# The short last slice of a dense layer: a bias written to PSUM by ScalarE and two row tiles for 64 features

## The chip, the cores and the metric

The kernel runs on one NeuronCore of a Trainium2 chip. The metric is the device time of one execution in microseconds (us), as the median of several runs. The engines are named as in the profile: PE is TensorE (matmuls), PEld its weight loads, ACT is ScalarE, DVE is VectorE, POOL is GpSimd and SP is SyncE, which issues most DMAs.

## What is computed

Two branches of the same input x (2048 tokens, D = 640 features) are mixed by a gate:

```
g = sigmoid((x * gate_w).sum(-1))                    # per token
a = 2*Re(C h_t) + x*Dskip,  h_t = L*h_(t-1) + B x_t  # complex diagonal recurrence, P = 640 states
b = gelu(x @ w1 + b1) @ w2 + b2                      # w1: 640 x 1728, w2: 1728 x 640
out = g*a + (1 - g)*b                                # bf16
```

The change is in the second product of b, `gelu(..) @ w2 + b2`. It sums over F = 1728 features, which are 13 slices of 128 and a last one of 64.

## The kernel before, in words

The tokens are worked in four quarters of 512 (q) and 16 chunks of 128 (c, four to a quarter). For each quarter the input stage makes, with matmuls of 512 columns (tokens), the 13 first-layer slices (`m1`, L640) and the ten B projections of the recurrence (`bproj`, L685), each a sum of five matmuls in one PSUM bank. ACT evicts a first-layer bank through the gelu into `Gl` (L648) and a B bank into `U` (L694). The last 64 features are made for two quarters at once by `m1_last` (L661): quarter q0 on output partitions 0 to 63, quarter q0+1 on 64 to 127, ten matmuls in all, and two gelus (L671) write them to rows 0 to 63 of two `GlL` tiles. Row 64 of each `GlL` holds ones.

DVE runs the recurrence in blocks of 256 tokens (`ssm(b)`: pre, scan, post), and post writes `H`, which holds two chunks. For each chunk then:

- `m2(c)`: the second layer in two halves of 320 columns, in banks 4 and 5. Each half is 13 matmuls of a `Gl` slice with w2 (L760) and one of `GlL` (L761), whose 65 rows are the 64 features and the ones; row 64 of the last w2 slice holds b2, so that this matmul also adds the bias. ACT evicts each half to `E1`, times 1 - g (L768).
- `cproj(c)`: the C projection, two halves of 320 columns in banks 6 and 7, ten matmuls of `H` with `CT` each (L786), which ACT evicts to `E2`, times g (L797). The last chunk has three pieces of 320, 192 and 128 columns and is finished by DVE straight from PSUM (L819).
- `comb(c)`: DVE adds x*Dskip*g (`xg`, L805), E1 and E2 (L489), and SP stores the result (L841).

`outs(q)` does this for the four chunks of a quarter, always `m2`, then `cproj`, then `comb`.

The order of the work on each engine is fixed when the program is built. A list scheduler (`Sched.order`) goes through time with an assumed cost for each step and takes, on the engine that is free first, the released step of the lowest `prio`; PE steps get rising numbers in program order. The cost is used for this order alone. Waits on semaphores are put in from the tiles and banks that steps read and write (`Prog.op`, `Emitter.wait`). Each engine then works through its own list strictly in order.

Banks: in the first two quarters the input stage goes round all eight banks (`in_bank`, L589), later round 0 to 3.

DMAs on SP's queue, in order: x for quarter 0, w1, b1, the B transposes, the xT transposes of quarter 1 (`xT1`), w2 in two pieces (`w2a`, 13 slices; `w2b`, the 64 rows; L579 and L580), the xT transposes of quarters 2 and 3 (`xT23`), and ten transposes of C (`CT`, L581). A reader of `CT` waits for all ten. On POOL's queue: b2 (one row, L852), Dskip and the gate weights (each repeated on 128 partitions), and x for later quarters.

Of the kernel before, what the change touches and what calls it, by code (L numbers as in the profile page):

```python
# [184 lines left out]
def bass_gated_mix__ssm_conv_s5__dense_activation_gelu__prompt_kernel(  # L185
# [40 lines left out]
    with ExitStack() as es, nc.Block() as block:  # L226

        def SB(name, shape, dt):
            return es.enter_context(nc.sbuf_tensor(name, list(shape), dt))
# [7 lines left out]
        Gl = [SB(f"Gl_{i}", [128, NF - 1, 512], BF16) for i in range(2)]  # L237
        GlL = [SB(f"GlL_{i}", [65, 512], BF16) for i in range(3)]
        dsk = SB("dsk", [128, D], BF16)
# [49 lines left out]
        BK_IN = [0, 1, 2, 3]  # L289
        BK_M2 = [4, 5]  # L290
        BK_C = [6, 7]
# [26 lines left out]
        def d_act(n):  # L318
            return 0.26 + n * 0.00084
# [68 lines left out]

        def f_ones():
            t = None  # L390
            for i in range(3):
                t = inc("dve", nc.vector.memset(GlL[i][64:65, :], 1.0))
            return t

        op("ones", "dve", 1.1, (), ["gl1"], f_ones, prio=-40)

# [182 lines left out]
        load("w2a", "sp", "l_w2a", W2sb[:, 0:NF - 1, :], B_w2[0:nmain, :].rearrange("(j p) d -> p j d", p=128), ["w2a"], prio=7.5, lat=8.0)  # L579
        load("w2b", "sp", "l_w2b", W2sb[0:FL, NF - 1, :], B_w2[nmain:F, :], ["w2b"], prio=7.6, lat=4.0)  # L580
        load_T("C", "l_C", [(CT[:, k, ci, :], (A_C_re, A_C_im)[ci][:, k * 128:(k + 1) * 128]) for k in range(KP) for ci in range(2)],  # L581
               ["CT"], prio=10, dur=14.0)

        ctr = {"in": 0, "pe": 0}

        def in_bank():
            i = ctr["in"]
            ctr["in"] += 1
            return (7 + i) % 8 if i < 2 * (NF - 1 + 2 * KP) + 1 - NW else BK_IN[i % 4]  # L589

# [62 lines left out]
        def m1_last(q0):  # L653
            jf = NF - 1
            bank = in_bank()

            def f_mm():
                t = None
                for k in range(KD):
                    for h in range(2):  # L660
                        t = nc.tensor.matmul(PS[bank][h * 64:(h + 1) * 64, :], W1sb[:, k, jf * 128:F],  # L661
                                             xT[:, k, (q0 + h) * 512:(q0 + h + 1) * 512], start=(k == 0), stop=(k == KD - 1))
                return inc("pe", t)

            op(f"m1_{q0}_{jf}", "pe", KD * d_mm(512) + 0.2, XT[q0] + XT[q0 + 1] + [("w1", "r")], [("bank", bank)], f_mm, prio=pe_prio())

            def f_ge():
                t = None
                for h in range(2):
                    ph = slice(h * 64, (h + 1) * 64)  # L670
                    t = inc("act", nc.scalar.activation(GlL[(q0 + h) % 3][0:64, :], PS[bank][ph, :], ACT.Gelu_apprx_tanh, bias=b1col[ph, jf:jf + 1]))  # L671
                return t

            op(f"ge_{q0}_{jf}", "act", 2 * d_act(512), [("bank", bank), "b1col"], [("glL", q0 % 3), ("glL", (q0 + 1) % 3)], f_ge, prio=10)

# [72 lines left out]


        def m2(c):  # L750
            q, t4 = c // 4, c % 4
            for hf in range(2):
                bank = BK_M2[hf]
                cols = slice(hf * HALF, (hf + 1) * HALF)

                def f_mm(bank=bank, cols=cols):
                    t = None
                    ts = slice(t4 * 128, (t4 + 1) * 128)
                    for jf in range(NF - 1):
                        t = nc.tensor.matmul(PS[bank][:, 0:HALF], Gl[q % 2][:, jf, ts], W2sb[:, jf, cols], start=(jf == 0), stop=False)  # L760
                    t = nc.tensor.matmul(PS[bank][:, 0:HALF], GlL[q % 3][0:FL + 1, ts], W2sb[0:FL + 1, NF - 1, cols], start=False, stop=True)  # L761
                    return inc("pe", t)

                op(f"m2_{c}_{hf}", "pe", NF * d_mm(HALF), [("gl", q % 2, jf) for jf in range(NF - 1)] + [("glL", q % 3), "gl1", "w2a", "w2b", "b2"],
                   [("bank", bank)], f_mm, prio=pe_prio())

                def f_ev(bank=bank, cols=cols):
                    return inc("act", nc.scalar.activation(E1[c % NE][:, cols], PS[bank][:, 0:HALF], ACT.Copy, scale=g1col[:, c:c + 1]))  # L768

                op(f"e1_{c}_{hf}", "act", d_act(HALF), [("bank", bank), ("g", q)], [("E1", c % NE, hf)], f_ev, prio=5)  # L770


        LAST = [(BK_C[0], 0, HALF), (BK_C[1], HALF, HALF + 192), (BK_M2[0], HALF + 192, D)]

# [70 lines left out]
        def outs(q):  # L845
            for c in range(4 * q, 4 * q + 4):
                m2(c)
                cproj(c)
                comb(c)

        m1_first()
        load("b2", "pool", "l_b2", W2sb[64:65, NF - 1, :], B_b2.rearrange("(o n) -> o n", o=1), ["b2"], prio=-30, dur=1.0, reads=["late"])  # L852
        load("dsk", "pool", "l_dsk", dsk[:, :], A_Dskip.partition_broadcast(128), ["dsk"], prio=-29, dur=1.0, reads=[("xT", 1)])
# [93 lines left out]
```

## Time and profile before

| | us |
|---|---|
| median of 3 runs | 217.36 (217.31 to 217.64) |
| profiled execution, its own time | 217.69 |
| its span, first to last instruction | 215.9 |
| PE busy | 212.0 (98% of the span) |
| DVE busy | 191.5 (89%) |
| ACT busy | 99.3 (46%) |
| 416 matmuls L760, 128x320: mean of one | 0.299 |
| 32 matmuls L761, 65x320: mean of one | 0.301 |
| 425 matmuls L640 and L685, 128x512: mean of one | 0.379 |
| gelu of a 128x512 bank (L648), one | 0.692 |
| eviction of 128x320 (L768), one | 0.528 |

Matmuls overlap in the pipeline, so the mean length of one is longer than the distance from one to the next; the distance is read from the chain of waits, which lists each stretch of the path with its start, its length and its number of instructions. The page has a strip of 40 slices for each engine, the groups of instructions by line, and the DMA issues; single stretches are read from the timeline. TensorE's granted clock is full (9 in each slice of the strip).

### The profile page before, as it was taken

The page shows a single profiled execution, that of the slowest core. Times are in us where ns is not written, and L with a number is a line of the kernel's source. Part 1 is how long each engine was busy: PE and PEld are TensorE (multiplying, and loading weights), DVE is VectorE, ACT ScalarE, POOL GpSimd, SP SyncE. Part 2 cuts the span into 40 slices and gives each one's busy share as a digit, 9 for nine tenths or more (in the row PEclk, how much of TensorE's full clock was granted, in tenths as well). Part 3 has the DMA queues.
Part 4 walks back from the last instruction along what each step waited for, and adds up shares of the span by engine and source line. Part 5 has one row for each costly group of instructions (what it writes and reads, how often), then busy time and mean ns, then how long its engine had stood idle before and what let it go on. Part 6 is the DMA issues. An engine that isn't in the chain of part 4 may idle for free.

```text
span 215.9 us, 3291 instructions
## 1 busy us (share of the span) xinstructions
PE 212.0 (98%) x1287; PEld 123.6 (57%) x1287; DVE 191.5 (89%) x269; ACT 99.3 (46%) x169; POOL 4.6 (2%) x13
## 2 busy tenths in 40 slices
PE   8899999999999999999999999999999999999995
PEld 3444444444567776444457777544447777777774
DVE  3989999999999999999996999799999999996313
ACT  2478556665533324556653322556662233233220
POOL 1010021000000100000000010000000000000000
PEclk9999999999999999999999999999999999999999
DMA  6987659996620050000000014000000000000000
GB/s 183 343 140 119 105 116 347 291 160 131 128 45 30 30 153 2 30 0 0 3 0 0 33 39 145 30 3 0 0 0 3 1 34 29 30 30 33 30 30 30
DMA packets 28201, 15.44 MB, mean 72 GB/s; under 512 B 22044, under 2 KB 27740, under 8 KB 28188
## 3 DMA queue, kind: packets, MB, share of 16 engines
q1 hardware_dynamic: 27598, 12.95, 25.4%
q0 software_dynamic: 560, 2.30, 3.4%
q8 instruction: 10, 0.16, 0.3%
q14 instruction: 3, 0.02, 0.0%
q10 hardware_dynamic: 30, 0.00, 0.0%
HBM read 7.38 MB, written 2.62 MB: 46 GB/s over the span
## 4 chain that ended last, share of the span: by engine, by line
PE 96%; DMA 2%; SPq 0%; DVE 0%; issue 0%
PE ps L760 26%; PE ps L640 22%; PE ps L786 20%; PE ps L685 20%; PE ps L621 4%; DMA W1sb<-in_B_w_dram 2%; PE ps L761 2%; PE ps L661 1%; SPq L330 0%; DVE osb L819 0%; PE ps L439 0%
## 5 line engine op out<-in xcount | busy, mean ns | idle before, releaser
L760 PE MATMUL ps<-W2sb,Gl 128*128 128x320 bf16 x416 | 61.4, 299 | 0.0
L760 PEld LDWEIGHTS ps<-W2sb,Gl 128*128 128x128 bf16 x416 | 40.6, 98 | 16.6 <-issue 0.4
L640 PE MATMUL ps<-xT,W1sb 128*128 128x512 bf16 x225 | 49.2, 379 | 0.0
L786 PE MATMUL ps<-CT,H 128*128 128x320 bf16 (+2 forms) x330 | 46.1, 295 | 0.0
L725 DVE TENSOR_TENSOR_SCAN W<-atab,V 128x1280 bf16<-128x1280 f32 x16 | 44.3, 2812 | 0.3
L685 PE MATMUL ps<-xT,BT 128*128 128x512 bf16 x200 | 43.8, 379 | 0.0
L786 PEld LDWEIGHTS ps<-CT,H 128*128 128x128 bf16 x330 | 31.7, 98 | 12.1 <-DMA CT<-in_A_C_im_dram 0.2
L648 ACT ACTIVATE Gl<-ps,b1col 128x512 bf16<-128x512 f32 x45 | 30.6, 692 | 16.1 <-PE ps L640 16.1
L640 PEld LDWEIGHTS ps<-xT,W1sb 128*128 128x128 bf16 x225 | 22.0, 98 | 26.6
L768 ACT ACTIVATE E<-ps,g1col 128x320 bf16<-128x320 f32 x32 | 16.9, 528 | 43.0 <-PE ps L761 43.0
L685 PEld LDWEIGHTS ps<-xT,BT 128*128 128x128 bf16 x200 | 19.5, 98 | 23.5 <-issue 0.4
L694 ACT ACTIVATE U<-ps 128x512 bf16<-128x512 f32 x40 | 23.9, 597 | 18.3 <-PE ps L685 18.3
L797 ACT ACTIVATE E<-ps,gcol 128x320 bf16<-128x320 f32 x30 | 15.8, 527 | 25.0 <-PE ps L786 25.0
L489 DVE TENSOR_TENSOR osb<-xg,E 128x640 bf16<-128x640 bf16 x15 | 7.3, 487 | 10.1 <-ACT E L797 10.0
L805 DVE SCALAR_TENSOR_TENSOR xg<-xn,gcol,dsk 128x640 bf16<-128x640 bf16 x16 | 13.9, 883 | 0.4
L600 DVE SCALAR_TENSOR_TENSOR scr<-xn,gwb 128x640 bf16<-128x640 bf16 x16 | 13.2, 822 | 0.4
L489 DVE TENSOR_TENSOR H<-H,V 128x1280 bf16<-128x1280 bf16 x16 | 12.5, 821 | 0.3
L489 DVE TENSOR_TENSOR V<-V,W 128x1280 bf16<-128x1280 bf16 x16 | 12.5, 821 | 0.3
L489 DVE TENSOR_TENSOR V<-mr,U 128x2560 bf16<-128x2560 bf16 x8 | 11.9, 1488 | 0.5 <-DVE s L489 0.2
L489 DVE TENSOR_TENSOR H<-c,W 128x2560 bf16<-128x2560 bf16 x8 | 11.9, 1488 | 0.1
L489 DVE TENSOR_TENSOR V<-s,W 128x2560 bf16<-128x2560 bf16 x8 | 11.9, 1484 | 0.0
L489 DVE TENSOR_TENSOR W<-mi,U 128x2560 bf16<-128x2560 bf16 x8 | 11.9, 1484 | 0.0
(84 smaller groups left out, 100.8 us busy)
## 6 DMA issues: line engine op xcount, KB each, us to landing
out_dram<-osb SPq DMA_DIRECT2D x15, 160.0 KB, 1.8
W2sb<-in_B_w_dram SPq DMA_DIRECT2D x1, 2080.0 KB, 12.6
xn<-in_A_x_dram POOLq DMA_DIRECT2D x3, 640.0 KB, 5.0
W1sb<-in_B_w_dram SPq DMA_DIRECT2D x5, 224.0 KB, 4.9
W1sb<-in_B_w_dram SPq DMA_DIRECT2D x1, 1040.0 KB, 7.8
xn<-in_A_x_dram SPq DMA_DIRECT2D x2, 320.0 KB, 3.4
xT<-in_A_x_dram SPq DMA_TRANSPOSE x10, 4.0
dsk<-in_A_Dskip_dram POOLq DMA_DIRECT2D x1, 160.0 KB, 6.8
```

The lines of the kernel that those rows point to most:

```text
L489: return inc("dve", nc.vector.tensor_tensor(out=o, in0=a, in1=b, op=o_))
L600: t = inc("dve", nc.vector.scalar_tensor_tensor(out=scr[:, :], in0=xn[q % 2][:, c, :], scalar=1.0, in1=gwb[:, :], op0=ALU.mult, op1=ALU.mu ...
L640: t = nc.tensor.matmul(PS[bank][:, :], W1sb[:, k, jf * 128:(jf + 1) * 128], xT[:, k, q * 512:(q + 1) * 512], start=(k == 0), stop=(k == KD ...
L648: return inc("act", nc.scalar.activation(Gl[q % 2][:, jf, :], PS[bank][:, :], ACT.Gelu_apprx_tanh, bias=b1col[:, jf:jf + 1]))
L685: t = nc.tensor.matmul(PS[bank][:, :], BT[:, kd, ci, k * 128:(k + 1) * 128], xT[:, kd, q * 512:(q + 1) * 512], start=(kd == 0), stop=(kd = ...
L694: return inc("act", nc.scalar.activation(dst, src, ACT.Copy, scale=1.0 if ci == 0 else -1.0))
L725: t = inc("dve", nc.vector.tensor_tensor_scan(out=g[:, ci, :], data0=a, data1=v[:, ci, :], initial=0.0, op0=ALU.mult, op1=ALU.add))
L760: t = nc.tensor.matmul(PS[bank][:, 0:HALF], Gl[q % 2][:, jf, ts], W2sb[:, jf, cols], start=(jf == 0), stop=False)
L768: return inc("act", nc.scalar.activation(E1[c % NE][:, cols], PS[bank][:, 0:HALF], ACT.Copy, scale=g1col[:, c:c + 1]))
L786: t = nc.tensor.matmul(PS[bank][:, 0:n], H[b % NHB][:, ci, k, s * 128:(s + 1) * 128], CT[:, k, ci, cols], start=(i == 0), stop=(i == 2 * K ...
L797: return inc("act", nc.scalar.activation(E2[c % NE][:, cols], PS[bank][:, 0:HALF], ACT.Copy, scale=gcol[:, c:c + 1]))
L805: return inc("dve", nc.vector.scalar_tensor_tensor(out=xg[c % 2][:, :], in0=xn[q % 2][:, c % 4, :], scalar=gcol[:, c:c + 1], in1=dsk[:, :] ...
```

## The change

- `GlL` becomes two tiles of 128 rows, one for two quarters. `m1_last` regroups the tokens: rows 0 to 63 get the first two chunks of both quarters, rows 64 to 127 the last two chunks of both. One gelu of 128 rows replaces the two.
- The bias is no longer a 65th row. b2 is loaded on 128 partitions (`b2b`), the rows of ones go, and ACT copies it into PSUM ahead of the matmuls (`seed`): the first 512 columns of the four chunks to banks 0 to 3, and the last 128 columns of two chunks each to banks 4 and 5. No second-layer matmul starts a sum of its own any more (`start=False`).
- The last w2 slice is loaded twice, on partitions 0 to 63 and 64 to 127 (`w2b0`, `w2b1`).
- For each quarter `m2_open` seeds the six banks and then runs the last 64 features of its four chunks (`m2l`): eight matmuls, alternately on array rows 0 to 63 and 64 to 127.
- `m2(c)` is the other 13 slices, in pieces of 512 and 128 columns instead of two of 320, and so are its evictions.
- In `outs(q)` the first chunk of each quarter has its C projection ahead of `m2_open` and `m2`.
- The input stage's last four banks of the first round become 0 to 3.

```diff
@@ -235,7 +235,8 @@
         BT = SB("BT", [128, KD, 2, P], BF16)
         CT = SB("CT", [128, KP, 2, D], BF16)
         Gl = [SB(f"Gl_{i}", [128, NF - 1, 512], BF16) for i in range(2)]
-        GlL = [SB(f"GlL_{i}", [65, 512], BF16) for i in range(3)]
+        GlL = [SB(f"GlL_{i}", [128, 512], BF16) for i in range(2)]
+        b2b = SB("b2b", [128, D], BF16)
         dsk = SB("dsk", [128, D], BF16)
         gwb = SB("gwb", [128, D], BF16)
         rows = SB("rows", [3 * KP, 128], BF16)
@@ -287,7 +288,6 @@
 
         PS = [es.enter_context(nc.psum_tensor(f"ps{i}", [128, 512], FP32)) for i in range(8)]
         BK_IN = [0, 1, 2, 3]
-        BK_M2 = [4, 5]
         BK_C = [6, 7]
 
         engines = {"sp": nc.sync, "act": nc.scalar, "dve": nc.vector, "pe": nc.tensor, "pool": nc.gpsimd}
@@ -386,13 +386,6 @@
 
         op("warm", "pe", 3.0, (), [("bank", 6)], f_warm, prio=-1000)
 
-        def f_ones():
-            t = None
-            for i in range(3):
-                t = inc("dve", nc.vector.memset(GlL[i][64:65, :], 1.0))
-            return t
-
-        op("ones", "dve", 1.1, (), ["gl1"], f_ones, prio=-40)
 
         def filler(name, n, prio, deps):
             def fn():
@@ -577,16 +570,21 @@
             load_T(f"B{ci}", f"l_B{ci}", [(BT[:, k, ci, :], (A_B_re, A_B_im)[ci][:, k * 128:(k + 1) * 128]) for k in range(KD)],
                    [("BT", ci)], prio=6.8 + 0.1 * ci, dur=6.6)
         load("w2a", "sp", "l_w2a", W2sb[:, 0:NF - 1, :], B_w2[0:nmain, :].rearrange("(j p) d -> p j d", p=128), ["w2a"], prio=7.5, lat=8.0)
-        load("w2b", "sp", "l_w2b", W2sb[0:FL, NF - 1, :], B_w2[nmain:F, :], ["w2b"], prio=7.6, lat=4.0)
+        for h in range(2):
+            load(f"w2b{h}", "sp", f"l_w2b{h}", W2sb[h * FL:(h + 1) * FL, NF - 1, :], B_w2[nmain:F, :], [("w2b", h)], prio=7.6 + 0.1 * h, lat=4.0)
         load_T("C", "l_C", [(CT[:, k, ci, :], (A_C_re, A_C_im)[ci][:, k * 128:(k + 1) * 128]) for k in range(KP) for ci in range(2)],
                ["CT"], prio=10, dur=14.0)
 
         ctr = {"in": 0, "pe": 0}
+
+        n_first = 2 * (NF - 1 + 2 * KP) + 1 - NW
 
         def in_bank():
             i = ctr["in"]
             ctr["in"] += 1
-            return (7 + i) % 8 if i < 2 * (NF - 1 + 2 * KP) + 1 - NW else BK_IN[i % 4]
+            if i < n_first - 4:
+                return (7 + i) % 8
+            return BK_IN[(i - n_first) % 4]
 
         def pe_prio():
             ctr["pe"] += 1
@@ -657,21 +655,18 @@
             def f_mm():
                 t = None
                 for k in range(KD):
+                    x4 = xT[:, k, q0 * 512:(q0 + 2) * 512].rearrange("p (q h t) -> p q h t", q=2, h=2)
                     for h in range(2):
-                        t = nc.tensor.matmul(PS[bank][h * 64:(h + 1) * 64, :], W1sb[:, k, jf * 128:F],
-                                             xT[:, k, (q0 + h) * 512:(q0 + h + 1) * 512], start=(k == 0), stop=(k == KD - 1))
+                        t = nc.tensor.matmul(PS[bank][h * 64:(h + 1) * 64, :].rearrange("p (q t) -> p q t", q=2), W1sb[:, k, jf * 128:F],
+                                             x4[:, :, h, :], start=(k == 0), stop=(k == KD - 1))
                 return inc("pe", t)
 
             op(f"m1_{q0}_{jf}", "pe", KD * d_mm(512) + 0.2, XT[q0] + XT[q0 + 1] + [("w1", "r")], [("bank", bank)], f_mm, prio=pe_prio())
 
             def f_ge():
-                t = None
-                for h in range(2):
-                    ph = slice(h * 64, (h + 1) * 64)
-                    t = inc("act", nc.scalar.activation(GlL[(q0 + h) % 3][0:64, :], PS[bank][ph, :], ACT.Gelu_apprx_tanh, bias=b1col[ph, jf:jf + 1]))
-                return t
-
-            op(f"ge_{q0}_{jf}", "act", 2 * d_act(512), [("bank", bank), "b1col"], [("glL", q0 % 3), ("glL", (q0 + 1) % 3)], f_ge, prio=10)
+                return inc("act", nc.scalar.activation(GlL[q0 // 2][:, :], PS[bank][:, :], ACT.Gelu_apprx_tanh, bias=b1col[:, jf:jf + 1]))
+
+            op(f"ge_{q0}_{jf}", "act", d_act(512), [("bank", bank), "b1col"], [("glL", q0 // 2)], f_ge, prio=10)
 
 
         def bproj(q):
@@ -747,30 +742,57 @@
             op(f"post{b}", "dve", 2 * d_dve(2560, 2) + 2 * d_dve(1280, 2), ["W", "ptab"], ["V", ("H", b % NHB)], f_post, prio=102 + 10 * b)
 
 
+
+        def piece(t4, i):
+            return (t4, slice(0, 512), slice(0, 512)) if i == 0 else (4 + t4 // 2, slice((t4 % 2) * 128, (t4 % 2 + 1) * 128), slice(512, D))
+
+        def m2_open(q):
+            for bank in (4, 5, 0, 1, 2, 3):
+
+                def f_seed(bank=bank):
+                    if bank < 4:
+                        return inc("act", nc.scalar.activation(PS[bank][:, :], b2b[:, 0:512], ACT.Copy))
+                    return inc("act", nc.scalar.activation(PS[bank][:, 0:256].rearrange("p (c d) -> p c d", c=2),
+                                                           b2b[:, 512:D].unsqueeze(1).broadcast_to([128, 2, 128]), ACT.Copy))
+
+                op(f"seed_{q}_{bank}", "act", d_act(512 if bank < 4 else 256), ["b2b"], [("bank", bank)], f_seed, prio=9)
+
+            def f_mm():
+                t = None
+                for i in range(2):
+                    for c in range(2):
+                        for h in range(2):
+                            bank, pc, dc = piece(2 * h + c, i)
+                            ph = slice(h * FL, (h + 1) * FL)
+                            t = nc.tensor.matmul(PS[bank][:, pc], GlL[q // 2][ph, (q % 2) * 256 + c * 128:(q % 2) * 256 + (c + 1) * 128],
+                                                 W2sb[ph, NF - 1, dc], start=False, stop=False, skip_group_check=True)
+                return inc("pe", t)
+
+            op(f"m2l_{q}", "pe", 0.75, [("glL", q // 2), ("w2b", 0), ("w2b", 1)], [("bank", b) for b in range(6)], f_mm, prio=pe_prio())
+
         def m2(c):
             q, t4 = c // 4, c % 4
             for hf in range(2):
-                bank = BK_M2[hf]
-                cols = slice(hf * HALF, (hf + 1) * HALF)
-
-                def f_mm(bank=bank, cols=cols):
+                bank, pc, dc = piece(t4, hf)
+                n = dc.stop - dc.start
+
+                def f_mm(bank=bank, pc=pc, dc=dc):
                     t = None
                     ts = slice(t4 * 128, (t4 + 1) * 128)
                     for jf in range(NF - 1):
-                        t = nc.tensor.matmul(PS[bank][:, 0:HALF], Gl[q % 2][:, jf, ts], W2sb[:, jf, cols], start=(jf == 0), stop=False)
-                    t = nc.tensor.matmul(PS[bank][:, 0:HALF], GlL[q % 3][0:FL + 1, ts], W2sb[0:FL + 1, NF - 1, cols], start=False, stop=True)
+                        t = nc.tensor.matmul(PS[bank][:, pc], Gl[q % 2][:, jf, ts], W2sb[:, jf, dc], start=False, stop=(jf == NF - 2), skip_group_check=True)
                     return inc("pe", t)
 
-                op(f"m2_{c}_{hf}", "pe", NF * d_mm(HALF), [("gl", q % 2, jf) for jf in range(NF - 1)] + [("glL", q % 3), "gl1", "w2a", "w2b", "b2"],
+                op(f"m2_{c}_{hf}", "pe", (NF - 1) * d_mm(n), [("gl", q % 2, jf) for jf in range(NF - 1)] + ["w2a"],
                    [("bank", bank)], f_mm, prio=pe_prio())
 
-                def f_ev(bank=bank, cols=cols):
-                    return inc("act", nc.scalar.activation(E1[c % NE][:, cols], PS[bank][:, 0:HALF], ACT.Copy, scale=g1col[:, c:c + 1]))
-
-                op(f"e1_{c}_{hf}", "act", d_act(HALF), [("bank", bank), ("g", q)], [("E1", c % NE, hf)], f_ev, prio=5)
-
-
-        LAST = [(BK_C[0], 0, HALF), (BK_C[1], HALF, HALF + 192), (BK_M2[0], HALF + 192, D)]
+                def f_ev(bank=bank, pc=pc, dc=dc):
+                    return inc("act", nc.scalar.activation(E1[c % NE][:, dc], PS[bank][:, pc], ACT.Copy, scale=g1col[:, c:c + 1]))
+
+                op(f"e1_{c}_{hf}", "act", d_act(n), [("bank", bank), ("g", q)], [("E1", c % NE, hf)], f_ev, prio=5)
+
+
+        LAST = [(BK_C[0], 0, HALF), (BK_C[1], HALF, HALF + 192), (BK_IN[0], HALF + 192, D)]
 
         def cproj(c):
             q, b, s = c // 4, c // 2, c % 2
@@ -844,12 +866,17 @@
 
         def outs(q):
             for c in range(4 * q, 4 * q + 4):
-                m2(c)
-                cproj(c)
+                if c % 4 == 0:
+                    cproj(c)
+                    m2_open(q)
+                    m2(c)
+                else:
+                    m2(c)
+                    cproj(c)
                 comb(c)
 
         m1_first()
-        load("b2", "pool", "l_b2", W2sb[64:65, NF - 1, :], B_b2.rearrange("(o n) -> o n", o=1), ["b2"], prio=-30, dur=1.0, reads=["late"])
+        load("b2", "pool", "l_b2", b2b[:, :], B_b2.partition_broadcast(128), ["b2b"], prio=-30, dur=1.0, reads=["late"])
         load("dsk", "pool", "l_dsk", dsk[:, :], A_Dskip.partition_broadcast(128), ["dsk"], prio=-29, dur=1.0, reads=[("xT", 1)])
         load("gwb", "pool", "l_gwb", gwb[:, :], gate_w.partition_broadcast(128), ["gwb"], prio=-28, dur=1.0, reads=[("xT", 1)])
 
```

## The prediction

> **What bounds the kernel now.** I read the page's busy line and its chain of waits first.
>
> ```profile
> PE 212.0 (98%) x1287; PEld 123.6 (57%) x1287; DVE 191.5 (89%) x269; ACT 99.3 (46%) x169; POOL 4.6 (2%) x13
> ...
> PE 96%; DMA 2%; SPq 0%; DVE 0%; issue 0%
> ```
>
> The chain that ends last is TensorE (PE) for 96%. From its first real matmul at 6.57 us to 213.4 us PE does not pause, so each nanosecond of PE work, and each PE pause, goes into the time one for one. Busy time says little of pace (matmuls overlap); I take pace from the chain in order of time (start, length, what):
>
> ```profile
> 45.81 1.20 PE ps L661 x10
> 47.01 10.90 PE ps L685 x50
> 57.91 1.77 PE ps L760 x13
> 59.67 0.14 PE ps L761
> 59.81 1.77 PE ps L760 x13
> 61.58 0.14 PE ps L761
> 61.72 2.77 PE ps L786 x20
> ```
>
> The reader is to see two things. L685 takes 216 ns per 512-column matmul (10.79 us for 50 in the later stages, 215.8), L760 and L761 136 ns per 320 columns; the 65-row L761 is as dear as a full one. And between the last input matmul (57.91) and the first C projection (61.72) lie 3.81 us of second-layer matmuls. Then I asked what that first C projection waits for. The weight loads at that point, the tile CT, and SyncE's queue:
>
> ```profile
> 61.59 0.25 PEld L786 LDWEIGHTS ps<-CT,H 128*128 128x128 bf16 x3 [0.21 <-DMA CT<-in_A_C_im_dram]
> ```
>
> ```profile
> DMA to landing us min/median/max: 3.0/3.6/3.7
> ```
>
> ```profile
> 29.54 1.54 SPq L330 DMA_DIRECT2D W2sb<-in_B_w_dram  x2
> 31.13 15.61 SPq L337 DMA_TRANSPOSE xT<-in_A_x_dram  x5
> 46.78 1.27 SPq L337 DMA_TRANSPOSE CT<-in_A_C_re_dram  x1
> ...
> 58.59 1.27 SPq L337 DMA_TRANSPOSE CT<-in_A_C_im_dram  x1
> ```
>
> The tenth CT transpose is issued at 58.59 and needs at least 3.0 us, so CT is complete at about 61.55; the load of L786 at 61.59 follows it, after a 0.21 us wait on that DMA. SyncE issues without a break from 0.74 to 59.86 us. CT is just in time today, and only because chunk 0's second layer covers 3.81 us.
>
> **What the Trainium skill says.** "TensorE: Matmul & The Clock Gate", Part 3 (what overlaps): matmuls on different row tiles start about 4 ns apart and run together. The trace has no row tiles, but L661's pairs on column tiles: ten matmuls in 1.20 us, 5 x 216 = 1.08 plus 0.12. "TensorEngine Tiling (Array Packing)", Key Properties: changing the tiling mode drains TensorE; those 0.12 us agree. The same TensorE page, Back-to-back issue gap, gives 81 ns for a 128-column matmul with its own weight load. Here the trace differs and decides:
>
> ```profile
> 212.67 0.44 PE L786 MATMUL ps<-CT,H 128*128 128x128 bf16 x5
> ...
> 213.17 0.22 PE L786 MATMUL ps<-CT,H 128*128 128x128 bf16 x1
> ```
>
> Of ten such matmuls, each with its own load, the first starts at 212.67 and the tenth at 213.17: 55.6 ns a step. Fourth, the TensorE page, Part 1: after an idle window of about 3.4 us the clock falls to half until a busy one has passed. The trace has no such pause in mid-run, only the start:
>
> ```profile
> 3.96 1.24 PE L412 MATMUL ps<-ident,xn 128*128 128x128 bf16 x10
> ...
> 5.23 0.73 PE L412 MATMUL ps<-ident,xn 128*128 128x128 bf16 x10
> ```
>
> Ten steps at about 105 ns, then ten at about 56: the slow pace held from 0.78 to about 5.1 us.
>
> **Part by part.**
>
> *Last 64 features.* Removed: 32 matmuls of L761, 8 per quarter of the tokens, 8 x 0.136 = 1.09 us each quarter. Added per quarter: two pairs of 512 and two of 128 columns. If pairs overlap, 2 x 0.216 + 2 x 0.056 = 0.54, plus one change of mode, 0.12 as at L661: 0.67. Gain 0.42 a quarter, 1.68 in all. Bounds: 2.2 with no switching cost; 0 or a loss of 0.5 if pairs do not overlap (4 x 0.216 + 4 x 0.056 = 1.09, plus the switch).
>
> *Other 13 slices.* 26 matmuls of 136 ns per chunk, 3.53 us, become 13 x 215.8 + 13 x 55.6 = 3.53. Gain under 0.1 in all: 0.08 by the unrounded steps (271.4 against 271.8 ns). At the skill's 81 ns it would be a loss of 208 x 25 = 5.3 us; I take the trace.
>
> *m1_last.* Same ten matmuls with tokens regrouped, and its gelu is one instruction instead of two (two take 1.39 us): nothing on PE, 0.7 us less on ScalarE (ACT), which has slack.
>
> *Seeds.* 24 ACT writes to PSUM. No row shows one; nearest are the 512-wide copies from PSUM (L694, 0.60 us) and a small table of 4 columns (0.20). Six a quarter: 4 x 0.60 + 2 x 0.40 = 3.2, 13 us in all, on an engine 46% busy. The E1 evictions change from two of 0.53 to about 0.60 + 0.30. Who waits: m2l waits for all six seeds, which wait for the banks' last evictions. Tightest is the second quarter, where the planned order gives m2l 20 C matmuls (2.72 us) as cover. There ACT has after m1_last, by its L671 start at 110.14, a queue of gelu, seed, gelu, seed: done about 1.6 us after PE leaves m1_last, 1.1 us to spare. Cost taken 0; at 0.9 us a seed the last would end about 1.2 us later, and PE would wait some 0.1. The other quarters have 30 C matmuls or a whole chunk as cover. Banks 0 to 3 are shared with the input stage; each is evicted 2 us or more before reuse: 0.
>
> *C before the second layer.* In the planned order PE comes from the last input matmul straight to c_0 (20) and half of c_1 (10), then m2l. c_0 waits for CT. Its 3.81 us of cover are gone. Nothing queued behind it on PE can pass it. So PE stops until CT is there: 3.81 us (57.745 to 61.55 by starts) plus 0.05 from landing to first matmul, plus whatever CT is late.
>
> *DMAs.* w2b is loaded twice: a further 80 KB on SyncE ahead of xT23 and CT. The first xT23 transpose already sits behind w2a's queue (five take 15.61 us, where a CT one takes 1.27), so I take the transfer alone: the page's 347 GB/s gives 0.23 us. Bounds: 0, or a full issue, 0.9 (the two W2sb issues take 1.54). b2b is 160 KB instead of 1.2 KB on GpSimd's queue, issued at 13.5 us beside the BT transposes: 0.1 taken, 0 to 0.5; xT1 lands about 0.8 us ahead of its use, BT too. CT so lands at about 61.9. Stall: 3.81 + 0.05 + 0.33 = 4.2 us, between 3.85 and 5.2.
>
> *DVE.* The memsets leave at the start, where PE waits for W1: 0. During the stall VectorE (DVE) waits some 6 us at the first combine, since chunk 0 is finished at about 70.9 instead of 65.1. The next H (4.5 us behind 1.9 of other work) is then ready at about 77.2; c_2 comes at about 78.7: 1.5 us left, cost 0. In the last quarter the planned order puts the combine of chunk 12 ahead of the last H; that leaves about 2.8 us before c_14. Tail: same three pieces, 0.
>
> *Sum.* -1.68 - 0.08 + 4.2 = +2.4 us. On the profiled execution, 217.69 us (span 215.9 and 1.8 around it), that is 220.1; its time is 0.33 above the median of 217.36, so the median becomes **219.8 us**.
>
> **Rivals.**
> - *Stall, and then a cold clock.* PE is idle some 4.2 us, more than the skill's window. If it re-starts at half speed for as long as at the start (4.3 us), it loses half of that: 219.8 + 2.2 = 222.0. For it: the pause is longer than one window. Against: windows run freely, so a whole one fits into 4.2 us only in about (4.2 - 3.4) / 3.4, one case in four.
> - *Pairs do not overlap, or 128-wide steps are load-bound.* No row tiles in the trace: 219.8 + 1.7 = 221.5 for the first, with 0.12 more per quarter for the switch already in. The second is 225.1; ten measured steps speak against it.
> - *Faster: CT is not the last to come.* Place: c_0's wait. If CT were complete when the input stage ends, at 57.75, only the PE gain is left: 217.36 - 1.76 = 215.6. It decides from a landing before about 59.5 us, where stall and gain are equal. Against: the last CT transpose is issued at 58.59 behind an unbroken queue, and nothing ahead of it was taken away; only a sudden change of transfer pace would do it.
>
> **How the numbers follow.** Stall with a warm clock 0.62, stall and cold clock 0.25, pairs not overlapping or slow 128-wide steps 0.07, CT early 0.06. Of the last, 0.04 end faster by over 0.2% and 0.02 within 0.2%, which is about what a measurement of this kernel can tell from no change; the rest, 0.94, is slower. The warm case runs from 217.36 - 2.3 + 3.85 = 218.9 to about 221; the cold one reaches from about 221.5 to 223. The range 218.9 to 222.8 leaves out the early CT, the slow 128-wide steps and the cold case's end.
>
> **What would show it.** Right: the chain has a DMA CT piece of about 4 us at 57.9; the weight load of the C line has one idle of that length; m2l's eight matmuls take 0.6 to 0.7 us with pairs starting within some ns; 128-wide steps of 56 ns; nothing waits for the seeds. Cold clock: steps of 270 ns for 320 columns after the stall. Wrong: no idle at c_0, or a PE wait for ACT at m2l, or DVE late at c_2.

## The result, and the profile after

| | before | after |
|---|---|---|
| median of 6 runs each, us | 217.52 (217.31 to 217.72) | 220.27 (219.39 to 224.04) |
| ratio, 95% interval | | 1.012 (1.008 to 1.016) |
| profiled execution, its own time | 217.69 | 219.51 |
| its span | 215.9 | 217.7 |
| mean granted TensorE clock, run by run | 1.0 in all | 1.0, 0.992, 0.992, 0.985, 1.0, 1.0 |

The ratio leaves out the run at 224.04 us, whose mean clock was 0.985. The kernel became slower, by about what was forecast. Behind the median lie two groups: three runs at full clock take 219.39 to 219.51 us, two at 0.992 take 221.03 and 221.26. The profiled execution is one of the first group, so the trace of after shows the loss without any loss of clock; the clock is followed up in the experiments.

The busy line and the shares of the chain of waits, after:

```profile
PE 210.5 (97%) x1287; PEld 112.5 (52%) x1287; DVE 190.2 (87%) x266; ACT 109.1 (50%) x191; POOL 4.6 (2%) x13
...
PE 71%; SPq 25%; DMA 1%; issue 1%; DVE 0%
```

PE is still busy for 97% of the span, but the chain was 96% PE before and is 71% now: SyncE's queue (SPq) holds 25%. That is not 25% of a loss. From the start until 60 us the chain simply runs along another engine that was just as busy, and it leaves that engine at one place only. In order of time (start, length, what):

```profile
57.26 3.07 DMA CT<-in_A_C_im_dram
...
60.46 4.24 PE ps L808 x30
64.70 0.67 PE ps L767 x8
...
65.50 7.22 PE ps L783 x52
```

This answers to the before chain with L760, L761 and L786 at 57.91. The last CT transpose lands at 60.33, the first C projection (L808) follows at once, and the row tiles (L767) and the second layer (L783) come behind it. The waits of after name the same place (us in total, times, longest):

```profile
DVE osb L482 <- ACT E L790: 6.6, 3, 4.6
...
PE ps L808 <- DMA CT<-in_A_C_im_dram: 2.8, 1, 2.8
```

PE waits for CT once, for 2.8 us. No PE wait for ACT's seeds is among the waits. DVE's 4.6 us is the combine of chunk 0, the wait forecast as "some 6 us". Now SyncE's queue of after (start, length, what is issued), to be held against the queue of before in the prediction:

```profile
5.87 7.69 SPq L337 DMA_TRANSPOSE BT<-in_A_B_re_dram  x5
...
27.81 2.17 SPq L330 DMA_DIRECT2D W2sb<-in_B_w_dram  x3
30.03 15.31 SPq L337 DMA_TRANSPOSE xT<-in_A_x_dram  x5
...
57.26 1.27 SPq L337 DMA_TRANSPOSE CT<-in_A_C_im_dram  x1
```

The three W2sb issues take 2.17 us where two took 1.54, so the second copy of the last w2 slice costs 0.63 us of issue. From the first of them to the last CT transpose it is 29.45 us, against 29.05 before. Nevertheless the last CT transpose is issued 1.33 us earlier than before (57.26 against 58.59). Most of the difference arises far upstream: the five transposes of B's real part hold the queue for 7.69 us here and held it for 9.78 before. The change does not touch them. The transposes ahead of CT don't take the same time in each execution, and it is not always the same ones that take longer: in a second profiled execution of this kernel (experiment 3) B's real part took 9.05 us and CT landed at 62.03; in the filler kernel of experiment 4, whose queue is the same, B's real part took 7.76, but xT23 16.66 instead of 15.31, and CT landed at 62.13. So this execution was an early one by about 1.7 us. The three full-clock runs of this measurement agree within 0.12 us, so the difference seems to lie between measurements more than between runs of one; what it comes from was not tested.

The row tiles, at the second quarter, in PE's timeline of after (start, length, what):

```profile
112.53 2.89 PE L808 MATMUL ps<-CT,H 128*128 128x320 bf16 x20
115.36 0.72 PE L767 MATMUL ps<-W2sb,GlL 64*128 64x512 bf16 x8
116.14 7.24 PE L783 MATMUL ps<-W2sb,Gl 128*128 128x512 bf16 x52
```

A length here includes the modelled end of the last matmul, so the cost is not in these lengths; it is in the distances between starts. The records of single matmuls give, in ns from each to the next:

```
last L808 -> first L767                 231   (pace of L808: 136)
within L767     4  222  3  213  3  53  3
last L767 -> first L783                 282   (pace of a 128-column step: 56)
column tiles, before's L661:
last L640 -> first L661                 309   (pace 216)
last L661 -> first L760                 312   (pace 216)
```

The pairs start 3 to 4 ns apart and do run together. The two edges are what was mis-sized: 95 ns more than the pace going in and 226 ns coming out, 0.32 us a quarter where 0.12 was put down.

### The profile page after: what moved, and what is told of

Its sections match the earlier page's. It is cut to its first block, busy times and chain, and to the rows that moved or that the text cites. A ratio compares the mean times of both kernels' runs of the same rounds, so it can differ in the third digit from the quotient of the medians.

```text
span 217.7 us, 3285 instructions
## 1 busy us (share of the span) xinstructions
PE 210.5 (97%) x1287; PEld 112.5 (52%) x1287; DVE 190.2 (87%) x266; ACT 109.1 (50%) x191; POOL 4.6 (2%) x13
## 4 chain that ended last, share of the span: by engine, by line
PE 71%; SPq 25%; DMA 1%; issue 1%; DVE 0%
PE ps L783 26%; SPq L337 22%; PE ps L808 20%; PE ps L638 13%; PE ps L680 10%; SPq L330 3%; DMA CT<-in_A_C_im_dram 1%; PE ps L767 1%; PE ps L660 1%; DVE osb L841 0%
## 5 line engine op out<-in xcount | busy, mean ns | idle before, releaser
L783 PE MATMUL ps<-W2sb,Gl 128*128 128x512 bf16 (+1 forms) x416 | 58.5, 299 | 0.4 <-PE ps L767 0.2
L808 PE MATMUL ps<-CT,H 128*128 128x320 bf16 (+2 forms) x330 | 45.9, 295 | 2.8 <-DMA CT<-in_A_C_im_dram 2.8
L783 PEld LDWEIGHTS ps<-W2sb,Gl 128*128 128x128 bf16 x416 | 32.6, 98 | 26.2 <-PE ps L767 0.7
L808 PEld LDWEIGHTS ps<-CT,H 128*128 128x128 bf16 x330 | 31.1, 98 | 14.6 <-issue 3.7
L790 ACT ACTIVATE E<-ps,g1col 128x512 bf16<-128x512 f32 (+1 forms) x32 | 16.8, 525 | 40.7 <-PE ps L783 40.2
## 6 DMA issues: line engine op xcount, KB each, us to landing
W1sb<-in_B_w_dram SPq DMA_DIRECT2D x5, 224.0 KB, 4.6
```

The source lines that it names most:

```text
L783: t = nc.tensor.matmul(PS[bank][:, pc], Gl[q % 2][:, jf, ts], W2sb[:, jf, dc], start=False, stop=(jf == NF - 2), skip_group_check=True)
L790: return inc("act", nc.scalar.activation(E1[c % NE][:, dc], PS[bank][:, pc], ACT.Copy, scale=g1col[:, c:c + 1]))
L808: t = nc.tensor.matmul(PS[bank][:, 0:n], H[b % NHB][:, ci, k, s * 128:(s + 1) * 128], CT[:, k, ci, cols], start=(i == 0), stop=(i == 2 * K ...
```

## The experiments

"c_0" is the kernel's first C projection. Times are medians with their range; a ratio is to the kernel before, measured beside it on the same chip, with its 95% interval.

### 1. Take the stall away, keep the rest: CT loaded ahead of xT23

```diff
-               ["CT"], prio=10, dur=14.0)
+               ["CT"], prio=7.85, dur=14.0)
```

> The changed kernel with one number altered: the ten CT transposes go ahead of the xT23 transposes on SyncE's queue, so that CT lands some 7 us earlier. The order on PE stays as in the changed kernel. If the whole loss is the wait of c_0 for CT (and what the clock does after it), no wait is left and only the gain on PE remains, 0.9 us by the two traces (1.76 by the forecast): 216.6, between 215.7 and 216.8, with the clock at 1.0 in every run. If the loss is in the new PE work itself (row tiles, 128-wide pieces, seeds), it stays above 218.

Measured: 216.33 us (216.16 to 216.44), ratio 0.9944 (0.9927 to 0.9961), clock 1.0 in all runs. The chain of this kernel (start, length, what):

```profile
53.37 4.05 PE ps L680 x18
57.42 4.08 PE ps L808 x30
61.50 0.67 PE ps L767 x8
```

CT is complete at 54.2 us, the input stage goes over into the C projection without a pause, and xT23 behind it is still early enough. So the rest of the change is a gain of 0.6%, and c_0's wait for CT is what turns it into a loss. From the start of c_0 to the last matmul it takes 154.52 us, as in after; in before the same work, from the first second-layer matmul on, takes 155.43. PE's gain is 0.91 us, not the 1.76 forecast.

The same edit in the kernel before:

> The kernel before with the CT transposes ahead of xT23, and nothing else. There CT came 0.05 us before it was needed, so an earlier one can gain at most some hundredths, and nothing if xT23 is still in time: 217.5. If the SyncE order brings a gain of its own, of which ct_early had its share, it falls by as much below 217.3.

Measured: 217.35 us (216.87 to 218.04), ratio 0.9979 (0.9966 to 0.9991). CT is complete at 54.3 there too, and it brings 0.2%. An early CT by itself is worth next to nothing; it is worth 4 to 7 us only to the order that needs it (220.27 in the first and 223.52 in a second measurement of the changed kernel, against 216.33).

### 2. The order alone

The kernel before, with nothing but this in `outs`:

```diff
-                m2(c)
-                cproj(c)
+                if c % 4 == 0:
+                    cproj(c)
+                    m2(c)
+                else:
+                    m2(c)
+                    cproj(c)
```

> The kernel before with one part of the change alone: in the first chunk of each quarter the C projection goes ahead of the second layer. If the wait for CT is the loss, this kernel has it without any of the gain: 217.5 + 3.0 to 4.2 = 220.5 to 221.7, and up to 2 us more in executions in which the clock falls. If the new PE work is the loss, it stays at 217.5.

Measured: 223.35 us (221.43 to 224.28), ratio 1.0255 (1.0218 to 1.0292); mean clock 1.0 in one run (221.43), 0.992 in three, 0.985 in two. The one run at full clock is 3.8 us above the kernel before, within the expectation for the stall alone. The others are above it by 0.9 to 2.9 us, and this is the first sign that a lost clock is common here and not one case in four. The window table of this kernel gives, for each stretch, its length, the busy time and count of PE, PEld, DVE, ACT and POOL, then PE's granted clock, the DMA share and GB/s:

```profile
59.00:61.00 2.00, 0.00 (x0) 0.00 (x0) 2.00 (x1) 0.00 (x0) 0.00 (x0) 1.00 0.74 151
61.00:63.00 2.00, 1.34 (x7) 0.86 (x8) 2.00 (x2) 0.00 (x0) 0.00 (x0) 0.75 0.01 1
63.00:65.00 2.00, 2.00 (x9) 1.13 (x8) 1.84 (x5) 0.53 (x1) 0.00 (x0) 0.50 0.00 0
```

CT lands at 61.57 and PE resumes at 61.66, still at full clock. The clock falls to half only at about 62.0, after work has begun again, and stays there for 13 steps of 267 ns instead of 136: 13 x 0.131 = 1.7 us.

### 3. The changed kernel again

> The changed kernel itself, unaltered, for the spread of its times. With the wait for CT and a clock that falls in some executions: two groups, about 219.4 to 221 at a mean clock of 1.0, and 221 to 224 at 0.992 or 0.985; the first group's own spread is that of the time at which CT lands. If the clock has no part, the times form one group that the clock doesn't order.

Measured: 223.52 us (222.71 to 223.66), ratio 1.0265 (1.0234 to 1.0296), mean clock 0.985 in three runs and 0.992 in two. This is the same kernel as after, at another time, and it lies above the first measurement and above the forecast range's top of 222.8. Of the two groups expected, the one at full clock did not appear. Its own profile shows why. PE's timeline (start, length, what, and in brackets the idle time before it):

```profile
62.17 6.68 PE L808 MATMUL ps<-CT,H 128*128 128x320 bf16 x30 [4.63 <-DMA CT<-in_A_C_im_dram]
```

Its windows, in the columns of the table above:

```profile
59.00:61.00 2.00, 0.00 (x0) 0.00 (x0) 2.00 (x1) 0.00 (x0) 0.00 (x0) 0.84 0.58 117
61.00:63.00 2.00, 0.83 (x4) 0.51 (x5) 2.00 (x2) 0.00 (x0) 0.00 (x0) 0.50 0.24 48
63.00:65.00 2.00, 2.00 (x9) 1.10 (x8) 1.85 (x5) 0.00 (x0) 0.00 (x0) 0.50 0.00 0
```

and after's, for the middle one of these stretches:

```profile
61.00:63.00 2.00, 2.00 (x17) 1.46 (x15) 2.00 (x2) 0.98 (x2) 0.00 (x0) 1.00 0.00 0
```

The same 30 matmuls of L808 take 6.68 us here and 4.24 in after. CT landed 1.7 us later, the pause was 4.63 us by the page instead of 2.80, the clock fell at about 60.4 during it (full until then, half after it gives the 0.84 of the first window), and 19 steps ran at half speed: 19 x 0.131 = 2.5 us. 1.7 and 2.5 make up the 4.1 us between the two profiled executions (spans 221.8 and 217.7).

### 4. A longer stall, and the same stall with PE kept busy

Four loads of 64x40 elements issued just ahead of CT, so that CT lands later:

```diff
+        junk = SB("junk", [64, 160], BF16)
...
+        for h in range(4):
+            load(f"junk{h}", "sp", f"l_junk{h}", junk[:, h * 40:(h + 1) * 40], B_w2[nmain:F, h * 40:(h + 1) * 40], [("junk", h)], prio=9 + 0.1 * h, lat=4.0)
```

> The changed kernel with four small loads (64 rows of 80 bytes, into a tile that nothing reads) on SyncE's queue ahead of the CT transposes, some 0.5 us of issue each, so that CT lands about 2 us later and PE pauses for 5 us instead of 3. If a longer pause lets the clock fall, most executions run at a mean clock of 0.985 to 0.992 and the profile shows half-speed steps after the pause: 219.4 + 2.0 + 1.7 to 3.3 = 223.1 to 224.7. If the pause has no effect on the clock: 221.4, clock 1.0.

Measured: 225.31 us (224.61 to 226.83), ratio 1.0363 (1.0334 to 1.0392), clock 0.985 in all six runs. The clock is as expected, the time is above the expected 223.1 to 224.7: the four loads hold the queue for 2.67 us instead of 2.0, and the queue reaches them at 47.67 us, late as in experiment 3, where it reaches CT at 47.25 (45.38 in the first profile). CT lands at 65.12. PE's timeline of this kernel (two lines were added above, so L808 is L811 here), and two of its windows:

```profile
65.25 6.80 PE L811 MATMUL ps<-CT,H 128*128 128x320 bf16 x30 [6.92 <-DVE W L723]
```

```profile
63.00:65.00 2.00, 0.00 (x0) 0.00 (x0) 2.00 (x1) 0.00 (x0) 0.00 (x0) 0.67 0.47 100
65.00:67.00 2.00, 1.75 (x7) 1.05 (x8) 0.66 (x5) 0.00 (x0) 0.00 (x0) 0.50 0.00 0
```

The releaser named is the scan on DVE; the scan feeds a later H and c_0 does not wait for it. CT's landing at 65.12, 0.13 us before the start, is the true one: a wait for several semaphores is put down to a wrong one here. Against the second measurement of the changed kernel CT lands 3.1 us later (65.12 against 62.03) and the span is 3.2 us longer: the time follows the landing one for one. With a pause of 6.9 us every run loses clock.

Then 13 matmuls on zeros into a free bank, between the last input matmul and c_0:

```diff
+                if c == 0:
+                    filler("fill", 13, pe_prio(), (), (ctr["b"],))
```

(Left out are the lines that note the last B projection in `ctr["b"]` and let `filler` wait for it.)

> The changed kernel with 13 matmuls of zeros into bank 6 (2.8 us, results not used) between the last input matmul and c_0, so that PE is not idle while it waits for CT. They cost nothing as long as CT lands later than 2.8 us after the input stage. If the runs above 219.5 us come from a clock that falls during the pause, they are gone: every run 219.4 to 220.3, granted clock 1.0. If they come from CT landing later in some executions, the spread of 219.4 to 221.3 stays, with the clock at 1.0 or not.

Measured: 221.27 us (220.89 to 221.65), ratio 1.0173 (1.015 to 1.0197), clock 1.0 in all five runs. PE's timeline:

```profile
57.16 3.01 PE L394 MATMUL ps<-const-float32-0.0 128*128 128x512 bf16 x13
62.22 2.88 PE L808 MATMUL ps<-CT,H 128*128 128x320 bf16 x20 [2.04 <-DMA CT<-in_A_C_im_dram]
```

CT lands at 62.13, as late as in the second measurement of the changed kernel (62.03), and c_0 starts at the same time. The useless work changes nothing in the wait, only PE's idle share of it (2.04 us instead of 4.63), and the clock stays. The time is 1.0 us above the top of what was expected, which took the landing of the first profile, 60.33. Against the second measurement it saves, by the ratios, 0.9%, about 2 us; the half-speed steps it avoids are 2.5. That separates the two costs: waiting for CT, and a clock that falls because PE was idle.

### 5. The seeds in the open

The forecast put the seeds at nothing, because the C projection covers them. Here CT is early and `m2_open` and `m2` come before `cproj`, in every chunk, held there by a dependency of each C projection on the chunk's own second layer (the lines that move CT and note the second layer's last step in `ctr["m2"]` are left out):

```diff
-                op(f"c_{c}_{hf}", "pe", 2 * KP * d_mm(c1 - c0), [("H", b % NHB), "CT"], [("bank", bank)], f_mm, prio=pe_prio())
+                op(f"c_{c}_{hf}", "pe", 2 * KP * d_mm(c1 - c0), [("H", b % NHB), "CT"], [("bank", bank)], f_mm, prio=pe_prio(), after=(ctr["m2"],))
...
-                    cproj(c)
                     m2_open(q)
-                    m2(c)
-                else:
-                    m2(c)
-                    cproj(c)
+                m2(c)
+                cproj(c)
```

> CT ahead of xT23 as in ct_early, and the second layer ahead of the C projection in each quarter, as in the kernel before, held by added dependencies. m2l then has nothing in front of it that covers the seeds. Forecast from the copies' 0.60 us: PE waits 1.4 to 1.7 us for the last seed in quarters one to three and not in the fourth, whose seeds are written during the third: 216.3 + 4 to 5 = 220.3 to 221.4. If seeds are cheaper or hidden some other way, it stays near 216.3.

Measured: 227.38 us (225.44 to 229.34), ratio 1.0433 (1.0396 to 1.047); clock 1.0 in the one run at 225.44 and below it in the others. A miss by 6 us over the top of the expectation (4 in the run at full clock), because the edit did more than was meant. PE waits for the seeds three times, as expected, but the added dependency also makes PE wait on a semaphore for its own last second-layer matmul ahead of each of the 16 C projections; and the clock fell. From the last L783 to the first L808 it is 279 to 280 ns at the least, where 56 is the pace without the wait, so the wait costs at least 0.22 us each, 3.6 in all. (The 0.18 in the next expectation is too low.) So the self-waits were taken out by a kernel of their own (number 6) and the experiment was made again with them gone:

> m2_first without PE's waits on its own matmuls; m2_first had, through the added dependencies, such a wait ahead of every C projection, 16 x 0.18 us. What is left over no_self_wait is then the seeds in the open: 5.9 us by the three pauses of m2_first (1.9, 1.9 and 2.1 us), so 215.8 + 5.9 = 221.7 in executions with the clock at 1.0, and 1.7 more in those at 0.992. If the seeds were not the cause of those pauses, it falls to 216.

Measured: 221.4 us (220.97 to 221.91), ratio 1.0176 (1.0151 to 1.0201), clock 1.0 in all four runs, as expected. Its chain at the second quarter:

```profile
108.40 0.70 ACT Gl L646
...
109.12 0.60 ACT ps L754
109.72 0.61 ACT Gl L646
...
112.20 0.61 ACT GlL L667
...
112.84 0.61 ACT ps L754
...
113.49 0.72 PE ps L767 x8
```

The path leaves PE and goes through ACT, gelu and seed in turn, which is just the queue the forecast described for this place. The three pauses are 1.8, 1.8 and 2.1 us beyond PE's pace, 5.7 in all, and 221.4 against 215.84 of the kernel below is 5.6. In the fourth quarter, where the row tiles still follow a C projection, there is no pause. Seeds cost nothing only while a C projection stands between the input stage and the row tiles.

### 6. What the row tiles cost at their edges

Theory: the exit of the row tiles contains a wait of PE on its own semaphore, besides the change of mode. PE runs its own list in order, so it is told to skip waits on its own earlier matmuls (all kernels here have CT early):

```diff
-                if myvc[prod] >= sq:
+                if myvc[prod] >= sq or engname == prod == "pe":
```

> ct_early without the semaphore waits of PE on its own earlier matmuls (PE works in order; the first 512-wide matmul of m2 is one that waits so for m2l). If that wait is what makes the step from m2l to m2 0.28 us and more, where 0.06 is the pace, the step falls to the cost of the mode switch, about 0.15, and the kernel gains 4 x 0.1 to 0.2: 215.5 to 215.9. If the drain of the mode switch alone makes the step, nothing changes: 216.3.

Measured: 215.84 us (215.46 to 216.09), ratio 0.9919 (0.9896 to 0.9943). The exit falls from 0.281 to 0.148 us (in the second and third quarter; both traces lack records at the other two), and from c_0's start to the last matmul it is 153.91 us instead of 154.52. Against the pace of 0.056 the exit that remains is 0.09, the entry 0.095, both of the size of the column tiles' edges in before (0.093 and 0.096).

The rival: the exit is long because the last, 128-column pair is too short to cover the load of the next weights. Then the 128-column pairs first should help:

```diff
-                for i in range(2):
+                for i in (1, 0):
```

> ct_early with the order inside m2l turned: the two pairs of 128 columns first, the two of 512 last. If only the mode switch drains PE, the 512-wide end hides most of it, as at m1_last, where the exit costs 0.10 over the pace: 216.3 - 4 x 0.15 = 215.7. If m2 waits for the end of m2l by its semaphore, the longer last matmul makes the step longer by what it gains: 216.3.

Measured: 216.6 us (216.11 to 217.19), ratio 0.9952 (0.9936 to 0.9968), no gain over experiment 1. The exit becomes 0.440 us and the row tiles ahead of it shorter by as much; last L808 to first L783 stays at 1.014 us. The rival falls. With both edits:

> no_self_wait and wide_last together. With the semaphore wait gone, only the mode switch is left between m2l and m2. If that drains the array, a 512-wide end costs as much over the pace as a 128-wide one (0.09 us by the 0.148 us step of no_self_wait) and the time is that of no_self_wait, 215.8; if a longer last matmul hides it, 4 x 0.09 less: 215.5.

Measured: 215.99 us (215.39 to 216.3), ratio 0.9928 (0.9908 to 0.9949): 0.881 us from L808 to L783, as without the second edit (0.880). Nothing is left there for it to gain.

### 7. Do pairs need the alternation?

The two inner loops exchanged, so that both matmuls of one row half are issued one after the other:

```diff
-                    for c in range(2):
-                        for h in range(2):
+                    for h in range(2):
+                        for c in range(2):
```

> ct_early with the loops in m2l exchanged, so that only one of four matmuls of a width finds its neighbour on the other row tile (the second of rows 0 to 63 and the first of rows 64 to 127). Row tiles that overlap give 2 steps for 4 matmuls when alternated and 3 here: 0.216 + 0.056 = 0.27 us more a quarter, 1.1 in all: 217.4. If row tiles did not overlap at all in the changed kernel, the order does not matter: 216.3.

Measured: 216.4 us (216.06 to 216.94), ratio 0.9947 (0.9927 to 0.9967), clock 1.0 in all runs. By the time alone this was to mean that pairs do not overlap even when alternated. The trace says the opposite: here too the eight matmuls start in pairs, 6 to 7 ns apart instead of 3 to 4, and the eight take 0.504 us instead of 0.501. So the pairs overlap in either program order, and the expectation was wrong in taking for granted that the order decides. It looks as if the second half's matmul starts past one of the first half that still waits for its rows. That is inferred: the records do not say which half a matmul belongs to. How far ahead it can reach was not tried.

## Why the prediction was right, and where its terms were off

It forecast 219.8 us for a stall with a full clock, 222.0 with a cold one, and slower with 0.94. The median is 220.27, inside the range of 218.9 to 222.8, and slower by 1.2%. The mechanism is the one put first: the second layer of chunk 0 covered the wait for CT, the change moves it behind c_0, and c_0 is nearly the whole loss. Experiments 1 and 2 show it from both sides.

On the profiled executions (spans 215.89 and 217.69), step by step:

| step | forecast, us | measured, us |
|---|---|---|
| last 64 features | -1.68 | -0.75 |
| 13 slices, and the rest of PE after c_0 | -0.08 | -0.16 |
| end of the input stage | 0 | -0.25 |
| stall at c_0 | +4.2 | +2.97 |
| sum | +2.4 | +1.8 |

*Last 64 features: the term that was mis-sized on PE.* Removing 32 steps of 0.136 us is right, 4.35 us. The row tiles take 0.878 us more than the step before them in three quarters and 0.967 in the first, 3.60 in all, where 4 x 0.67 = 2.67 was forecast. The "one change of mode, 0.12 as at L661" was read from a piece of the chain, ten matmuls in 1.20 us. That piece runs from the first L661 start to the next line's first start and so contains the exit alone; the entry, 0.093 us, hides in the end of the L640 piece ahead of it. Four entries are 0.38 us. The other part, 0.13 us at each exit and 0.53 in all, is PE's wait on its own semaphore, which the forecast did not see: an accumulation that goes on in the same banks is a dependency of PE on itself. Experiment 6 shows this part alone. What the Trainium skill says in "TensorEngine Tiling (Array Packing)", Key Properties, that a change of mode drains TensorE, agrees with the traces: 0.095 us over the pace going in and, without the self-wait, 0.09 coming out.

*13 slices.* Steps of 216 and 55 to 56 ns, as taken from the trace of before. The skill's 81 ns ("TensorE: Matmul & The Clock Gate", Back-to-back issue gap) is again not what these 208 matmuls do, each with its own weight load.

*Stall.* The cover lost is right: the wait starts where the input stage ends. The landing was forecast at 61.9 us; it was 60.33 in the profiled execution and 62.03 in the second one. The stall of 2.97 us is below the forecast's own bounds for it, 3.85 to 5.2. The forecast asked what the change adds to the queue (0.33 us), and not by how much this queue varies from one execution to the next. The two errors, 1.2 us less stall and 0.93 us less gain on the row tiles, largely cancel, and the input stage ended 0.25 us earlier. That the full-clock runs at 219.45 are so close to 219.8 is luck: with a landing at 62.13, near the forecast's, and a full clock, the filler kernel of experiment 4 takes 221.27. That the median lies in the range is luck in part as well, since the second measurement of the same kernel, 223.52, does not.

*Cold clock.* It was a rival with a chance of 0.25. It came in three of the first six runs, in all five of the second measurement, in five of six with the order alone and in all six with the longer stall. The price was put at 2.2 us, and 1.7 to 2.5 was found. The times with it, 221.0 to 224.0, lie around the rival's 222.0.

The skill's account of a window that runs freely ("TensorE: Matmul & The Clock Gate", Part 1) agrees with the clock that the traces record. From the moment at which the clock first goes full, which differs from trace to trace, each stretch up to the next change is a whole number of 3.41 us: 58.03 us, 17 of them, up to the fall with the order alone, and 54.61, 16 of them, in the second measurement of the changed kernel. The half-speed stretches are one such window (62.00 to 65.42 us with the order alone) or two (60.36 to 67.19 in the second measurement), which give the mean clocks of 0.992 and 0.985. The reason given against the rival, that a whole idle window fits into such a pause only in one case of four, did not hold: the window need not be idle as a whole. Counted on this grid, the window before the fall held 0.34 us of PE's work with the order alone, where the clock fell 0.3 us after PE had resumed, and 0.42 us in the second measurement. In after the pause of 2.80 us lies across an edge of the grid, at 58.75, and the clock stayed. How much work in a window keeps the clock stays open: in experiment 5's first kernel a window with 1.47 us of work, around a pause of 1.77 us, was followed by a fall, and a later one with 1.36 us was not; the same pauses in its second kernel, and 2.04 us in the filler, never were.

*Seeds.* At nothing, and right while covered. A seed takes 0.60 us, as taken. In the second quarter the last one ends at 114.31 and the row tiles start at 115.36: 1.05 us to spare, where 1.1 was forecast.

*DVE.* Right: the combine of chunk 0 waits 4.6 us, the next H is ready at 75.97 and c_2 starts at 77.45, 1.5 us later as forecast. PE waits for no H.

*The other rivals.* Pairs that do not overlap and slow 128-column steps are out by the starts of single matmuls. (The price of the first was reckoned too low: without overlap a quarter takes 2 x 0.216 + 2 x 0.056 = 0.54 us more, 2.2 in all, which makes 222.0 and not 221.5.) CT early did not happen by itself; made to happen, it gives 216.33, not 215.6, because of the smaller gain on PE.

What the experiments offer as a version better than both kernels is the change with CT ahead of xT23, 0.9944 (0.9927 to 0.9961), and the same with PE's self-waits left out, 0.9919 (0.9896 to 0.9943).

## What to carry to other kernels

Before moving a step earlier, look up for each of its inputs when it arrives and what covered the wait so far; where a transfer was just in time, reorder its queue in the same change, or the gain goes into a wait. Price such a wait twice, as time and as TensorE's clock afterwards (here one or two windows of 3.41 us at half speed), and ask how much the arrival varies between executions. The price of an edge between two kinds of work is read from starts on both sides of it, not from one piece of the chain.

## What the runs showed of the hardware that was not expected

- A change between full array and row or column tiles costs about 0.09 us in each direction, for both kinds.
- A wait of PE on its own last matmul costs 0.13 us at the row tiles' exit and 0.22 or more ahead of a C projection, although the list is in order anyway.
- The granted clock fell to half within a pause, or 0.3 us after it, and stayed there for one or two windows of 3.41 us, 13 to 19 steps, 1.7 to 2.5 us of loss. A window in which PE had worked for a tenth of the time (0.34 of 3.41 us) was followed by the fall. With thirteen matmuls on zeros in the pause it did not fall in five runs out of five.
- Transposes that the change does not touch moved CT's landing by 1.7 to 1.8 us between executions of the same queue: the five of B's real part held it for 7.69 and 9.05 us, the five of xT23 for 15.31 and 16.66.
- Traces with PE x1264 instead of x1287 lack matmul records. There, some steps read twice the pace (0.432 us for 512 columns), and an exit of the row tiles read 0.507 us where the complete trace of after has 0.281. The count on the busy line has to be looked at before a single long step is given a cause.
